# A gated convolution mixer on one core: the first filter half by column halves, one row block moved between filter loads

## The chip, the cores and the metric

The kernel runs on one core of a Trainium2 chip. The metric is device time in microseconds (us) of one launch. The engines are TensorE (PE, with its weight loads PEld), VectorE (DVE), ScalarE (ACT), GpSimd (POOL) and SyncE (SP); SP issues most of the DMAs, GpSimd the accumulating ones, ScalarE two small ones.

## What is computed

With S = 2048 rows and D = 640 columns, x = `A_q`:

```python
g = sigmoid((x * gate_w).sum(-1, keepdims=True))
# a: the gated long convolution
k_shift = sum_t k_pad[:, t:t+S] * shift_k[:, 3 - t]     # 4 taps
kv = k_shift * v
y  = irfft(rfft(kv_pad, 2S) * rfft(ssm_k_pad, 2S))[:S]  # per column
y  = y + kv * ssm_D
a  = x * y
# b: token-mixing MLP on the normalised rows
h = layernorm(x)
u = gelu(einsum("bsd,sf->bdf", h, w1) + b1)             # F = 1536
b = (einsum("bdf,fs->bds", u, w2) + b2).transpose
out = g * a + (1 - g) * b
```

All inputs and the output are bfloat16.

## The kernel before

**The convolution** is done with a short Fourier transform by matmuls. Rows are split by position into two halves (h = 0, 1) and four phases (p = 0 to 3). A transform of 1024 points becomes matmuls with cosine and sine tables `FTB[:, p, kt, c, k2, :]`, where c is the component (cosine or sine), k2 one of two blocks of frequencies and kt one of two blocks of 128 rows. The tables are made at the start: VectorE builds integer phases (`pint`, lines 801 to 808), ScalarE takes their sine (`sins`, line 810), one table of 1024 columns for each p, in the order 0, 2, 1, 3. Results lie in tiles `C[0..3]` and `SS` with four slots of `SL` = 2560 columns, a slot being (c, k2, 640 columns).

**The filter** `ssm_k` is stored by column of the model, so it is first transposed on TensorE: `transp(h, db)` (line 838) turns 128 of the 640 columns for one half, into one PSUM slot, and ScalarE evacuates the slot to `wT` (128x1024). Five of these (db = 0 to 4) make one half. Columns 0 to 319 of `wT` come from db = 0, 1 and 2. For h = 0, `fwd` (line 854) then makes, for every p, k2 and c, one group of four matmuls of 320 columns: two `kt`, each with the two column halves (`ci`) in the two halves of a PSUM slot. ScalarE evacuates each group (128x640) to `C[0]`. There are 16 such groups. Before each group of transposes of h = 0 TensorE does some matmuls on zeros (`spin`, `SPIN`), three more before the first group of `fwd`.

**The MLP** needs normalised rows. `X` holds `A_q` in four blocks of 640 KB (hk = 0 to 3), 16 tiles in all. VectorE takes statistics of each tile (`ln_tile`, line 913), GpSimd makes 1/sqrt of the variance for eight tiles at a time (`ln_scale`, line 926), VectorE applies it (`ln_apply`). The first MLP matmul (`m1`, line 1074; weights in `ring`) accumulates over hk, the second (`m2`, line 1112; weights in `W2`) fills the rest of the program. GpSimd also makes the tap matrices `KF` (line 971), four products that read `cw`, which ScalarE evacuates from a small transpose, and that are made to wait for the last integer phases of `pint` (`xr=[pv3]`).

**Later** the spectra of kv are multiplied by those of the filter (`product`, line 1138; `cross`, line 1178) on VectorE, with GpSimd's DMAs adding partial products in place, `invmix` mixes them for the inverse, and `inverse` (line 1209) multiplies by the inverse tables and by `A_q`. `q_hi` serves first as scratch for the products; afterwards the first 1024 rows of `A_q` are loaded into it anew (line 1262), as two DMAs of 640 KB. `q_lo` (line 1268) gets the other rows.

**What sets the order.** The program is written as a list of operations with read and write regions. A planner, `_Sched.run` (line 384), simulates the engines with durations given in the code (DMA: bytes by `rate`, 365 KB/us unless given, one transfer after another, plus 2 us) and picks on each free engine the ready operation with the lowest `prio` (its index in the program unless given). The order that comes out is emitted; each engine then runs its instructions strictly in that order, waiting on semaphores that `_Tracker` places from the regions touched. PSUM is four slots of two banks, `pp0` to `pp3`. A group takes a slot when its first matmul is planned (lines 450 to 453) and gives it back after its evacuation. The planner lets the convolution (`cv`) hold three at once and the MLP (`mlp`) two. Loads marked `chain=True` are issued by SP in program order (lines 765 to 817): the filter's h = 0 in three parts (256, 512 and 512 KB), X in four, small rows, the filter's h = 1, and then the ring and the key rows.

Of the kernel before, what the change touches and what calls it, by code (L numbers as in the profile page):

```python
# [18 lines left out]
class _Tracker:  # L19
# [230 lines left out]
        self.dma_sems[name] = sem  # L250
        self.dma_cnt[name] = 0

    def dma(self, stream, out_ap, in_ap, semname, transpose=False, noncontig=False, accum=False):
        reads = [in_ap] + ([out_ap] if accum else [])
        writes = [out_ap]
        acc = self.pre(stream, reads, writes)
        engobj = self.eng[stream]
        sem = self.dma_sems[semname]
        if transpose:
            ins = engobj.dma_start_transpose(out_ap, in_ap)  # L260
        elif accum:
            ins = engobj.dma_start(out_ap, in_ap, accum_op=ALU.add, max_dma_last_dim=2560)  # L262
        elif noncontig:
            with self.nc.allow_non_contiguous_dma(reason="tiny"):
                ins = engobj.dma_start(out_ap, in_ap)
        else:
            ins = engobj.dma_start(out_ap, in_ap)  # L267
        ins.then_inc(sem, 16)
        self.dma_cnt[semname] += 16
        v = self.dma_cnt[semname]  # L270
        self.dma_hist[(semname, v)] = dict(self.known[stream])
        src = ("dma", semname, v)
        for reg, mode in acc:
            self.add_record(reg, mode, src)
        return v
# [48 lines left out]
class _Sched:  # L324
# [59 lines left out]
    def run(self):  # L384
# [30 lines left out]
        while started < n:  # L415
            while frees and frees[0][0] <= t:
                _, sl, cls = heapq.heappop(frees)
                nfree.append(sl)
                held[cls] -= 1
            nxt = []  # L420
            progress = False
            for e in engs:
                while pend[e] and pend[e][0][0] <= t:
                    _, p, i = heapq.heappop(pend[e])
                    heapq.heappush(ready[e], (p, i))
                if free[e] > t:
                    nxt.append(free[e])
                    continue
                skipped = []
                pick = None  # L430
                while ready[e]:
                    p, i = heapq.heappop(ready[e])
                    op = ops[i]
                    if op.vt is not None and op.vt.slot is None:
                        c = op.vt.cls
                        if not nfree or held.get(c, 0) >= self.limit.get(c, 99):
                            skipped.append((p, i))
                            continue
                    pick = op
                    break  # L440
                for s in skipped:
                    heapq.heappush(ready[e], s)
                if pick is None:
                    if pend[e]:
                        nxt.append(pend[e][0][0])
                    continue
                op = pick
                progress = True
                started += 1
                if op.vt is not None and op.vt.slot is None:  # L450
                    nfree.sort()
                    op.vt.slot = nfree.pop(0)
                    held[op.vt.cls] = held.get(op.vt.cls, 0) + 1
                op.start = t
                if e in ("SP", "QA") or op.lat < 0:
                    issue = 1.2 if e == "POOL" else 0.1
                    s = max(t + issue, dma_free)
                    dma_free = s + op.dur
                    op.end = dma_free + 2.0 + (6.0 if e == "POOL" else 0.0)
                    free[e] = t + issue  # L460
                else:
                    op.end = t + op.dur
                    if op.lock:
                        op.end += max(port["POOL" if e == "DVE" else "DVE"] - t, 0.0)
                        port[e] = op.end
                    free[e] = op.end
                order.append(op)
                if op.vt is not None:
                    op.vt.left -= 1
                    if op.vt.left == 0:  # L470
                        heapq.heappush(frees, (op.end + 0.05, op.vt.slot, op.vt.cls))
                for s in op.asucc:
                    avail[s] = max(avail[s], op.start)
                    s.ndep -= 1
                    if s.ndep == 0:
                        heapq.heappush(pend[s.eng], (avail[s], s.prio, s.idx))
                for s in op.succ:
                    lat = 0.08 if s.eng == e else 0.15
                    if e == "PE" and s.eng == "PE":
                        lat = 0.0  # L480
                    avail[s] = max(avail[s], op.end + lat)
                    s.ndep -= 1
                    if s.ndep == 0:
                        heapq.heappush(pend[s.eng], (avail[s], s.prio, s.idx))
                nxt.append(free[e])
            if not progress:
                c = [x for x in nxt if x > t]
                if frees:
                    c.append(frees[0][0])
                assert c, "schedule stuck: " + str([(o.name, o.eng, o.ndep) for o in ops if not hasattr(o, "end")][:12])  # L490
                t = min(c)
# [19 lines left out]
def _build(nc, A_q, A_k, A_v, A_shift_k, A_ssm_k, A_ssm_D, B_x, B_w1, B_b1, B_w2, B_b2, gate_w, out):  # L511
# [6 lines left out]
    SL = 4 * D  # L518
# [3 lines left out]
    with ExitStack() as es:  # L522
# [179 lines left out]
        def dma(o, i, nbytes, stream="SP", prio=None, sem=None, rate=365.0, chain=False, **kw):  # L702
            if sem is None:
                sem = f"d{ndma[0]}"
                ndma[0] += 1
            if sem not in T.dma_sems:
                T.add_dma_sem(sem, es.enter_context(nc.semaphore(f"s_{sem}")))
            rd = [i] + ([o] if kw.get("accum") else [])
            o_ = SC.add(stream, nbytes / rate / 1000.0, lambda s: T.dma({"QA": "ACT"}.get(stream, stream), o, i, sem, **kw), rd, [o], prio=prio, lat=-1.0, name="dma")
            if chain:  # L710
                if last[0] is not None:
                    o_.after.add(last[0])
                last[0] = o_
            return o_

        def dr(t, off, ap):
            return bass.AP(tensor=t.tensor, offset=t.offset + off, ap=ap)
# [7 lines left out]
        def chk(ci):  # L725
            return lambda s: s[:, ci * 512:ci * 512 + 320]

        def ssm_load(h, a, b):
            dma(ssm[:, a:b, 1024 * h:1024 * h + 1024], dr(A_ssm_k, 128 * S * a + 1024 * h, [[S, 128], [128 * S, b - a], [1, 1024]]), 128 * (b - a) * 2048, chain=True)

        def row8(t, hk):
            return dr(t, (1024 * (hk // 2) + 4 * (hk % 2)) * D, [[8 * D, 128], [1, 4 * D]])
# [2 lines left out]
            return 16 + 128 * (1 - hk % 2)  # L735

        def x_load(hk):
            dma(X[:, hk, :, :], dr(A_q, 512 * hk * D, [[4 * D, 128], [1, 4 * D]]), 128 * 5120, chain=True)

        def w1_load(c, hk):  # L740
            dma(ring[c % 2][:, 4 * hk:4 * hk + 4, :], dr(B_w1, 512 * hk * F + 512 * c, [[4 * F, 128], [F, 4], [1, 512]]), 128 * 4096, chain=True)
# [24 lines left out]
        SSM1 = ((0, 2), (2, 5))  # L766
        small(Drow[:, :], dr(A_ssm_D, 0, [[0, 1], [1, D]]), 1280, "QA")
        small(rows[0:20, 0, 0:128], dr(A_shift_k, 0, [[128, 20], [1, 128]]), 5120, "QA")
        for a, b in SSM0:
            ssm_load(0, a, b)  # L770
        for hk in range(4):
            x_load(hk)
        small(rows[0:4, 1, :], dr(B_b2, 0, [[512, 4], [1, 512]]), 4096, "SP", chain=True)
        small(rows[0:12, 2, 0:128], dr(B_b1, 0, [[128, 12], [1, 128]]), 3072, "SP", chain=True)
# [4 lines left out]

        zz = alloc("zz", [128, 512], BF16, at=base_of(GTB))  # L780
        memset("DVE", zz[:, :], 0.0, prio=-1)
        SPIN = (6, 1, 1, 1, 1)

        def spin(k):
            return [((lambda s: s[:, 0:512]), zz[:, 0:128], zz[:, :], True, True)] * k
# [52 lines left out]
        def transp(h, db):  # L838
# [11 lines left out]
            o_ = act(V(wT, 2 * h * SL + 128 * db, [[SL, 2], [D, 4], [1, 128]]), (lambda s: s[:, :].rearrange("q (a b c) -> q a b c", a=2, b=4)), ACT.Copy, vt=vt, name="wT")  # L850
            if h == 0:
                o_.after.add(sins[0 if db == 0 else 2])

        def fwd(src, h, p, dst, slot, scale, name, neg=lambda c, k2: False):
            for k2 in range(2):
# [84 lines left out]
        lnlast = []  # L940
        kfirst = []
        KFP = (0, 5, 10, 15)
        srcW = lambda h: (lambda kt, p, ci: wT[:, 2 * h + kt, p, 320 * ci:320 * ci + 320])
        for h in range(2):
            for db in range(ND):
                transp(h, db)
            if h == 0:
                consts()
            if h in (1,):
                fwd_even(srcW(h), h, C[h], 1.0 / 1024.0, h == 1, "W")  # L950
            for p in (PORD if h not in (1,) else PORD[2:]):
                if h == 0 and p in (1, 3):
                    sins[p].prio = SC.ops[-1].idx - (16.5 if p == 1 else 8.5)
                fwd(srcW(h), h, p, C[h], p, 1.0 / 1024.0, "W", (lambda c, k2: False) if h == 0 else (lambda c, k2: c == 1))
            if h == 0:
                for t in range(8):
# [301 lines left out]
        lastp = []  # L1258
        chained(product, A1[1], A1[1], V0[1], tmp_of(q_hi, 0), V1[1])
        chained(product, A1[0], A1[0], V0[0], tmp_of(q_hi, 1), V1[0])  # L1260
        for kt in range(2):
            dma(q_hi[:, kt, :, :], dr(A_q, 512 * kt * D, [[4 * D, 128], [1, 4 * D]]), 128 * 5120)
        acc_dma(A1[1], V1[1])
        acc_dma(A1[0], V1[0])
        chained(product, A0[1], A0[1], V0[1], H(V0[1], 0))
        chained(product, A0[0], A0[0], V0[0])
        for kt in range(2):
            dma(q_lo[:, kt, :, :], dr(A_q, (1024 + 512 * kt) * D, [[4 * D, 128], [1, 4 * D]]), 128 * 5120).after.add(w2last)
# [41 lines left out]
```

## Time and profile before

| | |
|---|---|
| median of 4 runs | 185.02 us (184.11 to 186.54) |
| the profiled execution's own time | 184.11 us |
| its span in the trace | 182.2 us |
| TensorE, VectorE, ScalarE, GpSimd busy | 172.9, 171.6, 117.4, 39.1 us |
| DMA | 43.49 MB, mean 239 GB/s |
| chain that ended last | PE 84%, ACT 10%, DMA 3% |

The span runs from the first to the last event of the trace; the 1.9 us beside it are before and behind. Busy shares are means over stages with different limits, so they only say which engines to look at. The order of time and the table of stretches say which of them a stage waits for. In the trace's rows, `L293` is the helper line for every matmul, `L669` for every ScalarE operation, `L625` for every two-input VectorE or GpSimd operation, so the tiles (out<-in) tell what an operation is. A row's bracket is the engine's idle time ahead of it and what ended it.

### The profile page before, as it was taken

Reading aid. Unit: us, or ns where it says so; the run is one execution under the profiler, and the core shown is the slowest. Engines: PE = TensorE matmul, PEld = TensorE weight load, DVE = VectorE, ACT = ScalarE, POOL = GpSimd, SP = SyncE. Lnnn points to the kernel's source line nnn. Section 1 sums busy time; section 2 is a strip of 40 time slices with the busy share of each in tenths; the row PEclk is TensorE's granted clock in tenths of the full one; section 3 lists DMA queues with packets and bytes.
Section 4 is the critical chain, followed back from the end, with each engine's and each line's share of the span. In section 5 each row is a group of like instructions: output and inputs, shape, how many; then the busy total and the mean of one; then the engine's idle time right before and its main releaser. Section 6 shows DMA issues by size and latency. Waiting matters only on the chain.

```text
span 182.2 us, 3317 instructions
## 1 busy us (share of the span) xinstructions
PE 172.9 (95%) x1373; PEld 126.7 (70%) x1374; DVE 171.6 (94%) x203; ACT 117.4 (64%) x176; POOL 39.1 (21%) x42
## 2 busy tenths in 40 slices
PE   7978998979999999999999999999999999999991
PEld 2644584576778777776777778888888887678670
DVE  7799895999999999999998999999999999999875
ACT  5799988799989988149999941231322313761660
POOL 4059704000000055000510110402535000054000
PEclk9999999999999999999999999999999999999999
DMA  5999999999999989997499969699999998279484
GB/s 157 391 414 371 389 250 226 305 415 263 160 249 290 163 214 229 240 230 170 117 237 251 275 151 342 149 222 335 226 192 253 245 207 241 117 113 237 82 288 144
DMA packets 38541, 43.49 MB, mean 239 GB/s; under 512 B 15867, under 2 KB 31360, under 8 KB 38528
## 3 DMA queue, kind: packets, MB, share of 16 engines
q1 hardware_dynamic: 33296, 32.16, 59.6%
q0 software_dynamic: 5200, 11.14, 34.6%
q8 instruction: 10, 0.16, 0.3%
q10 hardware_dynamic: 32, 0.01, 0.0%
q14 instruction: 3, 0.02, 0.0%
HBM read 25.87 MB, written 2.62 MB: 156 GB/s over the span
## 4 chain that ended last, share of the span: by engine, by line
PE 84%; ACT 10%; DMA 3%; DVE 1%; issue 0%; DVEq 0%; SPq 0%
PE pp L293 84%; ACT C L669 4%; DMA ssm<-in_A_ssm_k_dram 3%; ACT wT L669 2%; ACT FTB L669 1%; ACT L669 1%; ACT ksh L669 1%; DVE cgb L625 0%; ACT cgb L669 0%; ACT GT L669 0%; DVE O L681 0%; DVE O L625 0%; DVEq L504 0%; SPq L267 0%; DVE cgb L639 0%
## 5 line engine op out<-in xcount | busy, mean ns | idle before, releaser
L625 DVE TENSOR_TENSOR C<-C 128x2560 bf16<-128x2560 bf16 (+2 forms) x37 | 54.6, 1521 | 0.8 <-DMA C<-SS 0.4
L293 PE MATMUL pp<-X,ring 128*128 128x320 bf16 x384 | 55.3, 299 | 0.0
L293 PE MATMUL pp<-GT,W 128*128 128x320 bf16 x384 | 52.8, 299 | 0.0
L293 PEld LDWEIGHTS pp<-GT,W 128*128 128x128 bf16 x384 | 43.4, 113 | 8.8 <-ACT cgb L669 0.2
L293 PEld LDWEIGHTS pp<-X,ring 128*128 128x128 bf16 x384 | 37.0, 98 | 15.1 <-DVE X L640 0.7
L669 ACT ACTIVATE C<-pp 128x640 bf16<-128x640 f32 x64 | 40.1, 725 | 5.4 <-PE pp L293 5.4
L669 ACT ACTIVATE O<-pp,c,omg 128x640 bf16<-128x640 f32 x15 | 13.3, 886 | 33.8 <-PE pp L293 33.8
L262 POOL DMA_DIRECT2D C<-C x8 | 10.9, 1611 | 46.5 <-DVE C L625 46.0
L293 PE MATMUL pp<-wT,FTB 128*128 128x320 bf16 x112 | 17.8, 300 | 1.6 <-ACT C L669 1.6
L669 ACT ACTIVATE cgb<-pp,gg 128x640 bf16<-128x640 f32 x16 | 12.7, 794 | 8.3 <-PE pp L293 8.3
L293 PEld LDWEIGHTS pp<-wT,FTB 128*128 128x128 bf16 x112 | 9.5, 98 | 8.8 <-ACT C L669 5.2
L919 DVE BATCH_NORM_STATS2 stats<-X 128x6 f32<-128x320 bf16 x32 | 13.7, 463 | 1.4 <-DMA X<-in_A_q_dram 1.4
L669 ACT ACTIVATE GT<-pp,cc 128x640 bf16<-128x640 f32 x12 | 9.4, 784 | 8.3 <-PE pp L293 8.2
L625 DVE TENSOR_TENSOR tm<-C,C 128x2560 bf16<-128x2560 bf16 (+1 forms) x7 | 14.3, 2057 | 0.0
L293 PE MATMUL pp<-C,FTB 128*128 128x320 bf16 x96 | 13.6, 299 | 0.0
L262 POOL DMA_DIRECT2D C<-q_hi x6 | 5.9, 977 | 31.2 <-DVE C L625 16.2
L293 PEld LDWEIGHTS pp<-C,FTB 128*128 128x128 bf16 x96 | 9.0, 98 | 4.1 <-ACT O L669 0.2
L669 ACT ACTIVATE gq<-gq 128x640 bf16<-128x640 bf16 x16 | 11.6, 729 | 0.3 <-DVE gq L625 0.3
L625 DVE TENSOR_TENSOR SS<-C 128x2560 bf16<-128x2560 bf16 x8 | 11.7, 1486 | 0.1
L625 DVE TENSOR_TENSOR C<-tm 128x2560 bf16<-128x2560 bf16 (+1 forms) x9 | 10.7, 1193 | 0.1
L669 ACT ACTIVATE wT<-pp 128x1024 bf16<-128x1024 f32 x10 | 9.5, 1034 | 1.2 <-PE pp L293 1.2
L293 PE MATMUL pp<-KF,KT 128*128 128x128 bf16 (+1 forms) x160 | 9.0, 213 | 1.2 <-ACT GT L669 1.1
(73 smaller groups left out, 186.8 us busy)
## 6 DMA issues: line engine op xcount, KB each, us to landing
ring<-in_B_w_dram SPq DMA_DIRECT2D x12, 512.0 KB, 10.2
W<-in_B_w_dram SPq DMA_DIRECT2D x12, 512.0 KB, 7.2
C<-C POOLq DMA_DIRECT2D x8, 640.0 KB, 11.5
X<-in_A_q_dram SPq DMA_DIRECT2D x4, 640.0 KB, 8.6
kn<-in_A_k_dram SPq DMA_DIRECT2D x4, 640.0 KB, 9.4
out_dram<-O SPq DMA_DIRECT2D x7, 320.0 KB, 2.8
C<-SS POOLq DMA_DIRECT2D x3, 640.0 KB, 11.7
ssm<-in_A_ssm_k_dram SPq DMA_DIRECT2D x3, 512.0 KB, 5.9
```

Of the source, the lines that this page charges most:

```text
L262: ins = engobj.dma_start(out_ap, in_ap, accum_op=ALU.add, max_dma_last_dim=2560)
L293: ins = self.nc.tensor.matmul(ps_ap, lhsT=lhsT, rhs=rhs, start=start, stop=stop, skip_group_check=True)
L625: o_ = SC.add(eng, d, lambda s: T.op(eng, lambda e: e.tensor_tensor(o, a, b, op), rd, [o]), rd, [o], prio=prio, name="tt")
L669: return T.op("ACT", lambda e: e.activation(o, src, func, **kw), rr + [src], ww)
L919: ops.append(SC.add("DVE", 0.38, (lambda o, i: lambda s: T.op("DVE", lambda e: e.bn_stats(o, i), [i], [o]))(o, i), [i], [o]))
```

## The change

1. The planner takes free PSUM slots in the order in which they came free; the list is no longer sorted.
2. In the chain of loads, block 0 of X is moved ahead of the last part of the filter's h = 0. The planner's rates for these loads are given anew (262 and 195 KB/us for the parts of h = 0, 385 for h = 1, 410 for X).
3. The filter's h = 0 goes through a new function, `fwd_c`: for each column half `ci`, each p and each k2, a group of four matmuls puts the two components c into the two halves of a PSUM slot, and one evacuation writes both. The loop over `ci` is outermost. `fwd` still serves h = 1.
4. Transposes db = 3 and 4 of h = 0, with their evacuations, and the sines of p = 1 and 3 get priority 0.
5. `SPIN` goes from (6, 1, 1, 1, 1) to (7, 3, 3, 2, 2).
6. The reload of `q_hi` is placed behind the product of `A0[1]` and waits for what is written to that tile's second component.

```diff
-    def dma(self, stream, out_ap, in_ap, semname, transpose=False, noncontig=False, accum=False):
-        reads = [in_ap] + ([out_ap] if accum else [])
+    def dma(self, stream, out_ap, in_ap, semname, transpose=False, noncontig=False, accum=False, wait=()):
+        reads = [in_ap] + ([out_ap] if accum else []) + list(wait)
...
                 if op.vt is not None and op.vt.slot is None:
-                    nfree.sort()
                     op.vt.slot = nfree.pop(0)
...
         def ssm_load(h, a, b):
-            dma(ssm[:, a:b, 1024 * h:1024 * h + 1024], dr(A_ssm_k, 128 * S * a + 1024 * h, [[S, 128], [128 * S, b - a], [1, 1024]]), 128 * (b - a) * 2048, chain=True)
+            dma(ssm[:, a:b, 1024 * h:1024 * h + 1024], dr(A_ssm_k, 128 * S * a + 1024 * h, [[S, 128], [128 * S, b - a], [1, 1024]]), 128 * (b - a) * 2048, chain=True, rate=(262.0 if a == 0 else 195.0) if h == 0 else 385.0)
...
         def x_load(hk):
-            dma(X[:, hk, :, :], dr(A_q, 512 * hk * D, [[4 * D, 128], [1, 4 * D]]), 128 * 5120, chain=True)
+            dma(X[:, hk, :, :], dr(A_q, 512 * hk * D, [[4 * D, 128], [1, 4 * D]]), 128 * 5120, chain=True, rate=410.0)
...
-        for a, b in SSM0:
+        for a, b in SSM0[:2]:
             ssm_load(0, a, b)
-        for hk in range(4):
+        x_load(0)
+        ssm_load(0, *SSM0[2])
+        for hk in range(1, 4):
             x_load(hk)
...
-        SPIN = (6, 1, 1, 1, 1)
+        SPIN = (7, 3, 3, 2, 2)
...
+        def fwd_c(p, ci, dst, scale):
+            for k2 in range(2):
+                vt = _VT("cv")
+                items = []
+                for kt in range(2):
+                    for c in range(2):
+                        items.append((chk(c), FTB[:, p, kt, c, k2, :], srcW(0)(kt, p, ci), kt == 0, kt == 1))
+                m_ = mms(vt, (spin(3) if (p, ci, k2) == (1 if EVH else 0, 0, 0) else []) + items, name="W")
+                m_.dur = 0.54
+                act(V(dst, p * SL + k2 * D + 320 * ci, [[2 * D, 2], [1, 320]]), two, ACT.Copy, vt=vt, name="We", scale=scale)
+
+        EVH = False
...
+        DB3 = 0
+        SINP = {1: 0, 3: 0}
...
                 transp(h, db)
+                if h == 0 and db > 2:
+                    for o_ in SC.ops[-2:]:
+                        o_.prio = DB3
...
-            for p in (PORD if h not in (1,) else PORD[2:]):
-                if h == 0 and p in (1, 3):
-                    sins[p].prio = SC.ops[-1].idx - (16.5 if p == 1 else 8.5)
+            if h == 0:
+                for ci in range(2):
+                    for p in PORD:
+                        fwd_c(p, ci, C[0], 1.0 / 1024.0)
+                for p in (1, 3):
+                    sins[p].prio = SINP[p]
+            for p in (() if h == 0 else PORD[2:]):
                 fwd(srcW(h), h, p, C[h], p, 1.0 / 1024.0, "W", (lambda c, k2: False) if h == 0 else (lambda c, k2: c == 1))
...
-        for kt in range(2):
-            dma(q_hi[:, kt, :, :], dr(A_q, 512 * kt * D, [[4 * D, 128], [1, 4 * D]]), 128 * 5120)
         acc_dma(A1[1], V1[1])
         acc_dma(A1[0], V1[0])
         chained(product, A0[1], A0[1], V0[1], H(V0[1], 0))
+        for kt in range(2):
+            dma(q_hi[:, kt, :, :], dr(A_q, 512 * kt * D, [[4 * D, 128], [1, 4 * D]]), 128 * 5120, wait=[H(A0[1], 1)])
         chained(product, A0[0], A0[0], V0[0])
```

More of the change, by code (lines that the diff above doesn't have):

```diff
@@ L707, in dma @@
                 T.add_dma_sem(sem, es.enter_context(nc.semaphore(f"s_{sem}")))
-            rd = [i] + ([o] if kw.get("accum") else [])
+            rd = [i] + ([o] if kw.get("accum") else []) + list(kw.get("wait", ()))
             o_ = SC.add(stream, nbytes / rate / 1000.0, lambda s: T.dma({"QA": "ACT"}.get(stream, stream), o, i, sem, **kw), rd, [o], prio=prio, lat=-1.0, name="dma")
```

## The prediction, before the changed kernel was run

> **What bounds the kernel now.** I read the page from the top, then the chain of waits, then a table of stretches cut where the matmul stream changes its nature, then VectorE, ScalarE and GpSimd in order of time over the first 40 us. First the page, busy shares:
>
> ```profile
> PE 172.9 (95%) x1373; PEld 126.7 (70%) x1374; DVE 171.6 (94%) x203; ACT 117.4 (64%) x176; POOL 39.1 (21%) x42
> ```
>
> TensorE and VectorE are both nearly full, so the few microseconds in which they stand still are what can be won. The chain of waits says where:
>
> ```profile
> 5.82 1.99 PE pp L293 x25
> 8.12 3.66 ACT wT L669 x4
> 11.79 1.03 ACT FTB L669
> 12.82 2.97 ACT C L669 x5
> 16.47 1.03 ACT FTB L669
> 18.15 11.44 PE pp L293 x102
> 38.81 137.71 PE pp L293 x1084
> ```
>
> From 38.81 us to 176.52 us it is one unbroken run of matmuls. Everything before it is a mixed start-up in which ScalarE (evacuations wT and C, sines FTB) sets the pace. The table of stretches (columns: stretch, length, then busy time and count of PE, PEld, DVE, ACT, POOL, granted clock, DMA share, GB/s):
>
> ```profile
> 5.80:11.40 5.60, 4.45 (x47) 3.26 (x49) 4.17 (x10) 5.01 (x7) 0.17 (x1) 1.00 1.00 410
> 11.40:22.10 10.70, 9.99 (x70) 5.47 (x69) 10.11 (x37) 10.70 (x19) 10.07 (x7) 1.00 1.05 386
> 22.10:29.10 7.00, 7.00 (x75) 5.80 (x73) 7.00 (x20) 6.04 (x8) 0.00 (x0) 1.00 1.12 259
> 29.10:38.80 9.70, 7.56 (x74) 4.50 (x72) 7.56 (x15) 8.12 (x12) 2.39 (x4) 1.00 1.03 303
> 38.80:176.50 137.70, 137.69 (x1086) 104.74 (x1087) 134.84 (x109) 83.65 (x131) 24.33 (x21) 1.00 0.95 219
> ```
>
> In 11.4 to 22.1 ScalarE is busy for all of it: the filter's first half is evacuation-bound. In 29.1 to 38.8 TensorE loses 9.70 - 7.56 = 2.14 us. After that it loses nothing, so a gain must be made before 38.8, by moving matmul work forward into the start, and it must not be lost again at the end. VectorE in order of time shows what holds the start:
>
> ```profile
> 9.26 0.49 DVE L919 BATCH_NORM_STATS2 stats<-X 128x6 f32<-128x320 bf16 x1 [1.36 <-DMA X<-in_A_q_dram]
> 10.40 0.68 DVE L639 TENSOR_SCALAR pint<-pint 128x1024 int32<-128x1024 int32 x1
> 21.38 2.23 DVE L640 TENSOR_SCALAR X<-X,mv,rstd 128x640 bf16<-128x640 bf16 x6 [0.56 <-POOL rstd L625]
> 31.52 2.94 DVE L640 TENSOR_SCALAR X<-X,mv,rstd 128x640 bf16<-128x640 bf16 x8 [2.11 <-POOL rstd L625]
> ```
>
> and GpSimd in order of time:
>
> ```profile
> 11.23 8.12 POOL L625 TENSOR_TENSOR KF<-cw,m 128x1120 bf16<-128x1120 bf16 x4 [8.44 <-DVE pint L639]
> 19.34 0.25 POOL L639 TENSOR_SCALAR sd<-mv 128x8 f32<-128x8 f32 x1
> ```
>
> The reader is to see a relay. VectorE waits 1.36 us for the first row block, with the last two integer operations of the phase table (pint) queued behind that wait. GpSimd's four tap products start only when the second of those is done (11.08), run 8.12 us, and the row statistics' root queues behind them (19.34 to 21.34), so VectorE waits another 0.56 us. The MLP matmuls can begin only at 22.27, and the second batch of rows is normalised only from 31.52.
>
> **The change part by part.**
>
> *Row block before the last filter load.* Before, X block 0 landed at 9.26 with 256 + 512 + 512 + 640 KB sent; the 768 KB ahead had landed at 5.77. That is 1152 KB in 3.49 us, 330 KB/us (estimate from these two landings). Block 0 moved ahead of the last 512 KB lands at about 5.77 + 640/330 = 7.7 us, and the third filter load at about 9.3. VectorE ends its previous operation at 7.89, so the 1.36 us go. The bytes ahead of every later load are the same, and SP issues the same number of descriptors, so blocks 1 to 3 and all weights land as before. Next in line: pint's end moves from 11.08 to about 9.3, the tap products to 9.4 to 17.5, the root to 17.5 to 19.4. Statistics for eight tiles (0.86 us each) are then ready at 17.65 - 1.36 = 16.3, and all twelve at about 19.4, so the 0.56 us go as well. First rows normalised at 19.5 rather than 21.38, second batch at 29.6 rather than 31.52. **VectorE is 1.9 us earlier.** The 2.11 us behind the second root stay: nothing else is ready there.
>
> *Column halves, both components per evacuation.* Counted: 16 groups of four 320-column matmuls and 16 evacuations of 128x640 as before; every matmul already has its own weight load (112 and 112). An evacuation stays at about 0.61 us (6.07 us for 10), a group of matmuls at 0.54. So zero of itself. What it does: the first half needs only the transposed columns 0 to 319, that is three of five transposes, so ScalarE has C work while the late third load arrives. Without this the block swap would cost: wT 3 and 4 can't be evacuated before 9.3 + 0.7. ScalarE's work from 5.18 to 23.45 is 18.27 us with one hole of 0.59 us (waiting for the tap transposes); it is conserved. The sines for the odd tables (1.15 us each) move to the front and can fill that hole: -0.6 to 0; I take -0.2.
>
> *Spins.* 17 in place of 10. The first extra one is cold: six took 2.74 us, so +0.43 us before the first transposes if the first filter rows are already there (their load is shown to land 2.7 us after issue, about 3.5); 0 to +0.4 on ScalarE's start. The others (0.22 us warm) sit where TensorE waits for data or slots (0.49 and 0.65 us at 9.4 and 10.9). I take +0.3 for all.
>
> *Slots in turn.* Before, the lowest free slot is taken, so three of four serve the filter. In turn, TensorE may run one evacuation further ahead: it can leave the evacuation-bound stage up to 0.6 us earlier, and a wait such as 1.07 us for the first gelu's slot (at 37.3) may fall on an older slot. Bounds: +0.5 (an in-order engine meets a slot freed later) to -1.6; by the nearer row, the group, I take -0.3.
> Here a rule speaks against the change. TensorE's row: 4.29 us for 28 matmuls from 18.15, with 0.21 us stops at each slot, at granted clock 1.00, 153 ns each. The Trainium skill, "TensorE: Matmul & The Clock Gate", section "A second HAM failure mode: psum-queue depth-cycling", says that cycling through PSUM banks each iteration makes the array stop briefly often enough that its clock swings between half and full. If it did, a group would take 1.08 us in place of 0.54, above the 0.61 of the evacuation: +0.47 x 16 = 7.5 us. By the trace, which already cycles three slots at full clock, 0. I take 0.
>
> *q_hi reloads later.* The two 640 KB loads were issued at 122.4 and 133.0; now both wait for the accumulate that C[1]'s second component gets. That was issued at 135.26 and takes 11.7 us (page, C<-SS), so they are issued at about 147. Queued behind them on SP is only q_lo (was 149.97, used at 170.9); the last W2 load (132.42) is ahead. Earlier loads took 3.6 to 10.7 us, giving 150.6 to 157.7 against first use at 158.04: hidden, with 0.3 to 7 us to spare. On the other side 1.28 MB leaves the window of the accumulates; the wait that it could shorten is 0.41 us on VectorE at 146.8, off TensorE's chain. I take 0; bounds -0.4 to +1.
>
> **Sum.** -1.9 (VectorE) -0.2 (sines) +0.3 (spins) -0.3 (slots) = -2.1 us. Does TensorE get all of it? The MLP matmuls of the first batch (34 until 29.1) start up to 1.9 us earlier but the array is full in 22.1 to 29.1. What pays is the second batch, ready at 29.6 instead of 31.5, just as TensorE begins to idle: of the 2.14 us lost there most are fillable. VectorE is moved as much, so the end, where the inverse follows VectorE by 0.9 us (first group 167.61, its input written by about 166.7), keeps its distance. Profiled execution 184.11 (span 182.2 plus 1.9) becomes 182.0; the median of the runs is 0.9 above it, so **182.9 us**.
>
> **Rivals.**
> - *Forecast, 0.50*: 182.9, own range 181.9 to 183.9 (half of the 2.1 us unfilled, or the gelu wait gone too).
> - *Absorbed, 0.24*: VectorE is early, but TensorE between 29 and 39 is paced by ScalarE (8.12 of 9.70 busy; two-matmul groups at 0.62 us each; a 1.28 us table load at 35.16), and only 0.3 to 0.8 us come through: 184.5. For it: four of the waits there are for C and for GT. Against: the array had no MLP work left just then.
> - *More, 0.05*: both the hole and the gelu wait close: 180.5.
> - *A wait in TensorE's fixed order, slower, 0.21*: the planner now believes 410 KB/us for row blocks, and places MLP groups from about 19.5 us between the filter's groups. If the tap products start as late as before (their taps' evacuation cw queued behind a sine, or behind the longer spins), rows are ready at 21.4 still. TensorE then stands 1.9 us with filter groups behind it, ScalarE starves once its stock of three groups (1.8 us) is used, and the second half's transposes and the second batch move too: +2 to +4 us, 187 to 189. It decides if the first normalised row comes over 0.6 us (a group) after its place in the order. The statement for it: 8.12 us of GpSimd work leave no slack before 19.34. A landing of q_hi past 160 would end alike and is counted here.
> - *That it doesn't do what it says*: the loads are chained in program order, so the swap is certain; I see none.
>
> **How the numbers follow.** What a measurement of this kernel can tell from no change is about 1%, 1.85 us; faster means below 183.17. Of the forecast's 0.50 about 0.41 lies below that and 0.09 above; with "more" 0.46 faster. Same: 0.09 + 0.24 = 0.33. Slower: 0.21. The range leaves out about a tenth at each end: 181.2 (past the forecast's own low end) to 187.2 (into the slow case).
>
> **What would show it.** Right: VectorE's first statistics before 8 us with no wait for X; tap products from about 9.4; first normalising near 19.5 and second near 29.6; unbroken matmuls from about 37 rather than 38.8. Wrong: ScalarE idle before 12 us (column halves don't cover the late load), TensorE waiting for X or the ring near 20 us, a wait for q_hi's load near 156 us, or the unbroken run starting at 38.8 again.

## The result, and the profile after

The changed kernel takes 184.34 us (median of 43 runs, 183.70 to 185.15), the kernel before 185.02 (64 runs beside them, 183.61 to 187.12). The ratio is 0.9962 [0.9949, 0.9976]: faster by 0.4%, clear of zero, and well short of the 1.1% that were forecast. The profiled executions are nearer still: 183.99 us after, 184.11 before, both with a span of 182.2.

Busy time of the engines, from the page of the kernel after:

```profile
PE 173.4 (95%) x1380; PEld 129.0 (71%) x1381; DVE 171.1 (94%) x203; ACT 117.1 (64%) x176; POOL 41.3 (23%) x42
```

TensorE is busy 0.5 us more, with seven matmuls more (the spins); GpSimd 2.2 us more, VectorE 0.5 and ScalarE 0.3 us less. The table of stretches, with the cuts of before:

```profile
5.80:11.40 5.60, 4.09 (x37) 2.46 (x37) 5.54 (x15) 5.60 (x8) 1.62 (x1) 1.00 1.02 413
11.40:22.10 10.70, 10.70 (x87) 7.23 (x85) 10.11 (x36) 10.07 (x18) 8.62 (x7) 1.00 1.05 384
29.10:38.80 9.70, 8.67 (x92) 6.07 (x91) 7.92 (x13) 8.63 (x12) 3.69 (x3) 1.00 1.01 263
38.80:176.50 137.70, 136.79 (x1073) 104.53 (x1070) 133.96 (x109) 82.84 (x132) 24.29 (x21) 1.00 0.93 220
```

From 29.1 to 38.8 TensorE is busy 1.11 us longer than before (8.67 against 7.56). In the last stretch, which lost nothing before, it now loses 0.91 us. VectorE in order of time:

```profile
19.94 2.94 DVE L639 TENSOR_SCALAR X<-X,mv,rstd 128x640 bf16<-128x640 bf16 x8 [0.56 <-POOL rstd L624]
30.07 2.94 DVE L639 TENSOR_SCALAR X<-X,mv,rstd 128x640 bf16<-128x640 bf16 x8 [2.11 <-POOL rstd L624]
...
143.74 4.30 DVE L624 TENSOR_TENSOR C<-C 128x2560 bf16<-128x2560 bf16 x3
147.95 1.49 DVE L624 TENSOR_TENSOR SS<-C 128x2560 bf16<-128x2560 bf16 x1
...
152.44 1.49 DVE L624 TENSOR_TENSOR SS<-C 128x2560 bf16<-128x2560 bf16 x1 [1.61 <-DMA C<-C]
153.85 4.29 DVE L624 TENSOR_TENSOR C<-C 128x2560 bf16<-128x2560 bf16 x3
```

and GpSimd:

```profile
9.78 8.13 POOL L624 TENSOR_TENSOR KF<-cw,m 128x1120 bf16<-128x1120 bf16 x4 [7.00 <-DVE pint L638]
17.89 0.25 POOL L638 TENSOR_SCALAR sd<-mv 128x8 f32<-128x8 f32 x1
```

The relay moved as foreseen: tap products 1.45 us earlier (9.78 for 11.23), normalising 1.44 us earlier (19.94 for 21.38; 30.07 for 31.52). The wait of 0.56 us for the root stayed. At the other end a wait of 1.61 us for an accumulating DMA is new; the one of before was 0.41 us, at another step:

```profile
144.91 1.49 DVE L625 TENSOR_TENSOR C<-C 128x2560 bf16<-128x2560 bf16 x1
146.82 7.10 DVE L625 TENSOR_TENSOR C<-C 128x2560 bf16<-128x2560 bf16 x5 [0.41 <-DMA C<-SS]
153.84 1.49 DVE L625 TENSOR_TENSOR SS<-C 128x2560 bf16<-128x2560 bf16 x1
```

VectorE reaches this place 1.17 us earlier (143.74 for 144.91), but its order has changed. `invmix` of the second half writes to `SS`. Two such steps (147.95 and 152.44) now stand among those of the first half, and the second of them needs the last accumulate. Before, the first step into `SS` stood behind all five into `C`. ScalarE over the first 24 us:

```profile
5.34 1.02 ACT L668 ACTIVATE wT<-pp 128x1024 bf16<-128x1024 f32 x1 [0.76 <-PE pp L293]
...
12.48 1.02 ACT L668 ACTIVATE wT<-pp 128x1024 bf16<-128x1024 f32 x1 [0.41 <-PE pp L293]
13.73 1.02 ACT L668 ACTIVATE wT<-pp 128x1024 bf16<-128x1024 f32 x1 [0.22 <-PE pp L293]
...
17.06 6.73 ACT L668 ACTIVATE C<-pp 128x640 bf16<-128x640 f32 x11
```

It begins 0.16 us later than before (5.18), stands still for 0.41 and 0.22 us until the last two groups of transposes are done (those of the third load), and ends the filter's first half at 23.79 (before: 23.45). TensorE:

```profile
10.50 0.72 PE L293 MATMUL pp<-wT,FTB 128*128 128x320 bf16 x4 [1.51 <-ACT wT L668]
...
16.59 5.66 PE L293 MATMUL pp<-wT,FTB 128*128 128x320 bf16 x40
22.14 1.25 PE L293 MATMUL pp<-X,ring 128*128 128x320 bf16 x8
...
107.50 43.63 PE L293 MATMUL pp<-GT,W 128*128 128x320 bf16 x320
158.29 2.33 PE L293 MATMUL pp<-C,FTB 128*128 128x320 bf16 x16 [0.62 <-DVE C L624]
...
176.22 1.79 PE L293 MATMUL pp<-GT,W 128*128 128x320 bf16 x12
```

and in the kernel before:

```profile
22.27 1.25 PE L293 MATMUL pp<-X,ring 128*128 128x320 bf16 x8
...
108.28 44.72 PE L293 MATMUL pp<-GT,W 128*128 128x320 bf16 x328
...
158.26 4.58 PE L293 MATMUL pp<-C,FTB 128*128 128x320 bf16 x32
...
176.34 1.79 PE L293 MATMUL pp<-GT,W 128*128 128x320 bf16 x12
```

Three times of TensorE tell the story. I call the first **T0**, the end of the filter's first half on TensorE: 22.14 us, 22.27 before. The second is the first m2 matmul: 107.50, 108.28 before. The third is the last m2 group: 176.22, 176.34 before. So the start is where it was, 0.65 us are won between T0 and m2, and 0.62 of the 0.78 in hand are lost at 158.29, where TensorE waits for VectorE. The chain of waits shows behind what:

```profile
135.54 16.44 DMA C<-C
...
152.44 0.98 DVE SS L624
...
153.85 4.30 DVE C L624 x3
...
158.29 18.10 PE pp L293 x132
```

One accumulate of 640 KB takes 16.44 us to land. That is not new: of the three accumulates issued in this window the slowest takes 16.4 us in the kernel before too, and the quickest 9.7 us where it took 11.5. What is new is that a step which needs the slowest stands ahead of those that TensorE waits for.

The profiles explain 0.12 us of the 0.68 between the medians. Much of the rest is in the spread: 28 of the 64 runs of before are above 185.15 us, none of the 43 after. The other 36 of before have a median of 184.59, only 0.25 above the median after (a cut at the highest run of after can only narrow the difference).

### The profile page after: what moved, and what is told of

Its sections match the earlier page's. It is cut to its first block, busy times and chain, and to the rows that moved or that the text cites. A ratio compares the mean times of both kernels' runs of the same rounds, so it can differ in the third digit from the quotient of the medians.

```text
span 182.2 us, 3334 instructions
## 1 busy us (share of the span) xinstructions
PE 173.4 (95%) x1380; PEld 129.0 (71%) x1381; DVE 171.1 (94%) x203; ACT 117.1 (64%) x176; POOL 41.3 (23%) x42
## 4 chain that ended last, share of the span: by engine, by line
DVE 47%; PE 24%; ACT 13%; DMA 9%; issue 5%; POOL 1%; DVEq 0%
DVE C L624 31%; PE pp L293 24%; DMA C<-C 9%; ACT gq L668 4%; DVE tm L624 4%; ACT FTB L668 2%; DVE q_hi L624 2%; DVE SS L624 2%; ACT C L668 2%; DVE gq L624 2%; DVE vkv L624 2%; DVE kv L624 2%; ACT wT L668 2%; ACT GT L668 1%; DVE kp L749 1%
## 5 line engine op out<-in xcount | busy, mean ns | idle before, releaser
L293 PE MATMUL pp<-wT,FTB 128*128 128x320 bf16 x112 | 17.3, 300 | 2.4 <-ACT wT L668 1.5
L293 PEld LDWEIGHTS pp<-wT,FTB 128*128 128x128 bf16 x112 | 10.3, 98 | 7.7 <-ACT C L668 2.1
L668 ACT ACTIVATE gq<-gq 128x640 bf16<-128x640 bf16 x16 | 11.7, 732 | 0.6 <-DVE gq L624 0.6
L262 POOL DMA_DIRECT2D O<-q_hi x4 | 4.8, 1200 | 28.4 <-DVE q_hi L624 28.4
```

The lines of the kernel that those rows point to most:

```text
L293: ins = self.nc.tensor.matmul(ps_ap, lhsT=lhsT, rhs=rhs, start=start, stop=stop, skip_group_check=True)
L668: return T.op("ACT", lambda e: e.activation(o, src, func, **kw), rr + [src], ww)
```

## The experiments

Ratios are to the kernel before, with 95% intervals. Most edits are to the kernel after. Three readings in competition: G, that the later reload of `q_hi` gives time back at the end; that the gain was never made, since the start is paced by ScalarE and its order; and W, that the moment at which the array reaches full speed decides.

**The end.** e1 puts the reload back:

```diff
+        for kt in range(2):
+            dma(q_hi[:, kt, :, :], ...)
         acc_dma(A1[1], V1[1])
...
-        for kt in range(2):
-            dma(q_hi[:, kt, :, :], ..., wait=[H(A0[1], 1)])
```

> The changed kernel with the q_hi reload back at its old place. Theory G (given back late): the reload, now issued at 143.9 us into the same window as the accumulates, makes the accumulate C<-C land late (152.0) and costs TensorE 0.62 us at 158.3; with the reload earlier that wait goes and the time is 183.6 to 183.9. Theory S (spread): the old reload, issued into the accumulates between 122 and 133 us, is what puts a share of the runs of before above 185.2; then this kernel has that upper group again and its median is 184.8 to 185.3. Theory N: the reload does nothing and the time stays at 184.2 to 184.5.

0.9992 [0.9959, 1.0025], 184.87 us (184.37 to 188.24). With the old place TensorE still waits 1.04 us for VectorE's C (at 152.41) and VectorE 1.08 us for an accumulate. G falls as the account of a loss: the later reload costs nothing and may be worth 0.3% (the intervals overlap). Four of the 14 runs are at 187.2 to 188.2, and their cause was not traced; without them the median is 184.65. The edit changes more than the load: VectorE's order at the end is that of before again, as in every profile with the old place (before, e1, e4, e8, e16). The changed order comes with the later place (e2, e3 and e6 have it too). Each order has its wait for an accumulate.

e5 keeps `q_lo` out of the window of the accumulates:

```diff
-            dma(q_lo[...], ...).after.add(w2last)
...
         Z1 = invmix(A1[0], A1[1], (SS, 0), None, None)
+            dma(q_lo[...], ..., wait=[V(C[3], 0, [[1, SL]])]).after.add(w2last)
```

> The changed kernel, the same order of instructions, but the two q_lo loads (1.28 MB, issued at 147.05 us) wait for VectorE's fourth inverse-mixing step on the second half. Theory: they share the DMA engines with the last accumulates, which land at 152.0 and hold VectorE 1.6 us and TensorE 0.62 us. Then both waits shrink and the ratio to the kernel before is 0.991 to 0.994. Rival: the accumulates are slow of themselves (their own queue), then the wait stays and the ratio is that of the changed kernel, 0.995 to 0.998, or worse if q_lo comes too late for its use at 170.8.

0.9968 [0.9946, 0.9990]. VectorE's wait for the accumulate is 1.55 us and TensorE's 0.57, and the slowest accumulate takes 16.4 us again: it is not slow because of this load.

e14 leaves out the last two accumulates (the sum of `V1[0]` into `A1[0]` is missing from the output):

```diff
-        acc_dma(A1[0], V1[0])
```

> The changed kernel without the last two accumulating DMAs of 640 KB (C<-C into A1[0]); the output leaves their sum out. If VectorE's wait for their landing (1.6 us at 150.8) is what makes TensorE stand 0.62 us at 158.3, both waits go and the time falls by 0.5 to 0.8 us against the changed kernel: ratio 0.991 to 0.994. If TensorE's wait there has another cause, it stays: 0.996.

1.0108 [1.0067, 1.0150]. The planner changed the order of VectorE's steps and issued the two loads of `q_lo` at 132.44 us, just ahead of the accumulate that is left there. This one then takes 13.4 us (9.7 in the changed kernel), VectorE waits 2.31 us for it and TensorE 2.27. So e14 does not isolate what it was made for. e11 tells the planner that accumulates take longer (in the kernel of e9, below):

```diff
-                    op.end = dma_free + 2.0 + (6.0 if e == "POOL" else 0.0)
+                    op.end = dma_free + 2.0 + (8.0 if e == "POOL" else 0.0)
```

> As e9, with the planner's latency of an accumulating DMA at 8 us in place of 6 (they take 10 to 16). The start keeps its order; TensorE gets 16 more second-MLP matmuls ahead of the first inverse, so it should no longer wait for VectorE near 157 us (0.6 to 1.1 us in the others). If that wait was what gave part of the lead back, the ratio is 0.003 to 0.006 below e9's; if the end is VectorE's chain (rival), it is the same as e9's or above.

1.0066 [1.0037, 1.0094]. The wait near 157 us is gone, but now all of m2 is done before the last inverse and nothing fills the gaps of the tail, and VectorE waits 1.57 us for `q_hi`. A gain of a microsecond ahead of 150 us is thus not simply passed on to the end. That VectorE's order and its accumulates set the time there is read from the traces; no run changes them alone.

**Slots in turn.** e2 sorts the free list again:

```diff
+                    nfree.sort()
                     op.vt.slot = nfree.pop(0)
```

> The changed kernel with the free slots sorted again. If the turn of slots gave TensorE its missing wait for the first gelu (1.07 us at 37.3 before, none after), it comes back and the time is 184.9 to 185.4. If it was the earlier rows that closed it (rival), 184.2 to 184.6.

1.0096 [1.0065, 1.0126], 187.38 us. TensorE in order of time in e2:

```profile
6.27 0.82 PE L293 MATMUL pp<-zz 128*128 128x512 bf16 x3 [1.11 <-ACT wT L669]
...
23.22 1.25 PE L293 MATMUL pp<-X,ring 128*128 128x320 bf16 x8
```

The second transposes get the slot of the first, so TensorE stands 1.11 us until ScalarE has emptied it; T0 is 1.08 us later than after. With this start, slots in turn are worth 1.3% (1.0096 against 0.9962). The profile is of e2's lower group of runs (8 at 185.3 to 186.2); the 14 above 187.2 have no profile, so the wait of 1.11 us explains only part of the 1.3%. e4 is e2 with the reload of e1, which leaves the start of the change alone:

> The kernel before with the start alone (load order, column halves, spins, priorities, rates). VectorE should be 1.4 us early at its second normalising (about 30.1 us). If the start carries the gain: 184.1 to 184.5, if it is the slots and the reload: 184.8 to 185.3.

1.0129 [1.0067, 1.0191], 187.84 us (6 runs). T0 is 25.05: the same wait of 1.11 us, and in its profile the array went on at half speed for some 3 us behind it (eight transposes took 1.07 us at 8.30 and 0.71 at 10.45). VectorE has no lead here: the tap products start only at 11.83, behind the late evacuation of `cw`, and the second batch is normalised at 32.12, not at the expected 30.1.

e3 is the kernel before with the two other parts, slots in turn and the later reload:

> The kernel before with the slots in turn and the later reload, without anything of the start (load order, column halves, spins, priorities). If the start carries the gain: 184.8 to 185.3. If the gain is the slots and the reload, as theory S has it: 184.1 to 184.5.

0.9995 [0.9970, 1.0019]: nothing. So the slots and the reload together are worth nothing to the old start (that neither does anything alone is not shown), and the new start needs the slots.

**The start, part by part.** e6 takes the row block back behind the filter loads:

```diff
-        for a, b in SSM0[:2]:
+        for a, b in SSM0:
             ssm_load(0, a, b)
-        x_load(0)
-        ssm_load(0, *SSM0[2])
-        for hk in range(1, 4):
+        for hk in range(4):
             x_load(hk)
```

> The changed kernel with the row blocks behind all three filter loads again, all else kept. VectorE should wait for X again (about 1.4 us) and normalise the second batch at about 31.5. If VectorE's lead is what TensorE gained from (the prediction's step), the unbroken run of matmuls starts 1.5 to 2 us later and the ratio is 1.003 to 1.008. If ScalarE paces TensorE there (rival), 0.995 to 0.999.

0.9922 [0.9899, 0.9946], 183.58 us: faster than the whole change. ScalarE in e6, then TensorE:

```profile
11.28 1.95 ACT L668 ACTIVATE wT<-pp 128x1024 bf16<-128x1024 f32 x2
...
16.08 6.74 ACT L668 ACTIVATE C<-pp 128x640 bf16<-128x640 f32 x11
```

```profile
21.17 1.22 PE L293 MATMUL pp<-ident,ssm 128*128 128x128 bf16 x16
...
157.52 2.33 PE L293 MATMUL pp<-C,FTB 128*128 128x320 bf16 x16 [1.08 <-DVE C L624]
```

The two holes in front of the last transposes are gone, the last C evacuations start 0.98 us sooner, T0 is 21.17, m2 begins at 106.30. The expected loss on VectorE did not come: it normalises at 19.70 and 30.49. The planner, which now takes the block to be later, put the last `pint` ahead of the statistics. The relay was freed by VectorE's order; the swap of the loads was not needed for it, and held up the transposes. The rates given anew are kept in e6, and by them the planner expects the block later than by the old ones; no run leaves them out, so their share in VectorE's order is not shown. Of the 1.20 us in hand at m2 against the whole change, 0.46 go into a longer wait for VectorE (1.08 for 0.62), and 0.70 come through (183.29 against 183.99 in the profiled executions).

e7 puts back 10 spins for 17:

```diff
-        SPIN = (7, 3, 3, 2, 2)
+        SPIN = (6, 1, 1, 1, 1)
```

> The changed kernel with the ten spins of before. If the spins only cost time, as the prediction has it, 0.3 us less: ratio 0.993 to 0.996. If they keep the array's clock from coming up late (theory W: where TensorE stood still at 5 to 7 us, in the sorted kernels, matmuls stayed at half speed until 9 us), some runs are 1 to 2 us longer, the spread grows past 2 us, and the median is 185 or more.

0.9915 [0.9889, 0.9942], 183.48 us. T0 is 21.49: the seven spins cost 0.65 us there. The lead is still 0.65 at m2 (106.85) and 0.35 at the last m2 group (175.87), since TensorE's wait for VectorE's C grows from 0.62 to 0.92 us. e8 adds them to the kernel before:

> The kernel before with the seventeen spins alone. By the cost alone 0.3 us more: ratio 1.001 to 1.003. By theory W the group of longer runs of before (above 185.2) goes and the ratio is 0.994 to 0.998. If with sorted slots the spins wait for the evacuation of the first transposes (1.1 us, as in the sorted kernels), 1.004 to 1.012.

1.0005 [0.9977, 1.0033]. T0 is 23.30 in its profile, 1.03 us later than before. Its 14 runs lie between 184.53 and 186.01, the 54 of the kernel before beside them between 183.91 and 187.09. That would fit spins that are dearer at best and cheaper at worst, but the extremes of so few runs don't show it.

e9 is e6 and e7 together:

> The changed kernel with both the row blocks behind the filter loads and the ten spins, so with slots in turn, sines and transposes early, column halves and the later reload. Theory T: the end of the filter's first half on TensorE (T0: 22.14 us in the changed kernel, 21.17 with the old load order, 21.49 with the old spins), paced by ScalarE, carries over to the end, and VectorE's lead doesn't. Then T0 is 20.5 to 20.9 and the ratio 0.985 to 0.990, less what VectorE's wait for the accumulates near 157 us takes (it grew to 1.08 us as TensorE got earlier), so 0.988 to 0.992. Rival, the prediction's step: the load order is what gives the gain, then 0.996 or more.

0.9953 [0.9921, 0.9984]: the gains do not add. Its runs fall into two groups, 9 at 182.99 to 183.44 and 11 at 184.18 to 185.67. Its profile is of the lower group, and even there the array is late:

```profile
6.35 1.07 PE L293 MATMUL pp<-ident,ssm 128*128 128x128 bf16 x8 [0.57 <-DMA ssm<-in_A_ssm_k_dram]
```

Eight transposes take 1.07 us here and at 8.00, and 0.72 at 9.99; in e6 and e7 they take about 0.7 from 6.0 on. T0 is 21.43, no earlier than in e6: what the fewer spins save is lost again at half speed.

e10 is e9, e12 the kernel after, without column halves:

```diff
-                for ci in range(2):
-                    for p in PORD:
-                        fwd_c(p, ci, C[0], 1.0 / 1024.0)
+                for p in PORD:
+                    fwd(srcW(h), h, p, C[h], p, 1.0 / 1024.0, "W")
```

> As e9, with the filter's first half by components again (no column halves). In e9 no evacuation of C stands before the last of wT, so the column halves should give nothing there: T0 within 0.3 us of e9's and a ratio within 0.003 of it. Rival: they are worth something of their own (1 us).

> The changed kernel by components (no column halves), all else kept, the row block still ahead of the third filter load. The prediction says that the swap would cost without the halves, since ScalarE has no C work until the late load is transposed: T0 0.6 to 1 us later than 22.14, ratio 1.000 to 1.005. If the halves do nothing here either: 0.995 to 0.998.

e10 is 0.9989 [0.9958, 1.0021], e12 0.9913 [0.9877, 0.9949] (183.87 us, 9 runs). So column halves seem to gain 0.4% with the block behind the filter (e9 against e10; the intervals overlap), and cost 0.5% with the block ahead of it (after against e12; the intervals just touch, and by the medians it is 0.25%), the very case in which I had called them needed. In e12 TensorE does wait 1.02 us for the third load, but its last two groups of transposes start at 9.97 and 11.20, and T0 is 21.37. In the kernel after a W group (four filter matmuls) with a wait of its own of 1.51 us (at 10.50) stands in front of the last two, and they start at 11.74 and 12.97. Behind T0 the profile of e12 doesn't show the gain: it is the slowest of its nine runs (184.42), with m2 at 108.04 and a wait of 1.83 us for VectorE's C.

**VectorE's lead by itself.** e13 is the kernel after with one statistics instruction done six times, which makes VectorE 2.1 us late and leaves all orders as they are:

```diff
+                nx = 6 if (t, ci) == (1, 1) else 1
-                ops.append(... T.op("DVE", lambda e: e.bn_stats(o, i), [i], [o]) ...)
+                ops.append(... [T.op("DVE", lambda e: e.bn_stats(o, i), [i], [o]) for _ in range(nx)] ...)
```

> The changed kernel with one row statistic (0.43 us) done six times in place of once, early on VectorE, every engine's order unchanged. VectorE then normalises at about 21.4 and 31.6 us, as before the change, while the end of the filter's first half on TensorE (T0, 22.14) can't move. If VectorE's lead was on the path, as the prediction has it, its 1.5 us come back as 1.3 to 1.5 us: ratio 1.003 to 1.005 to before. If T0 alone counts, 0 to 0.3 us: 0.996 to 0.998. Between: the part that came through.

> The changed kernel once more, beside e13, e14 and the kernel before on the same chip: 0.995 to 0.998, all runs within about 1.5 us of each other.

e13 is 1.0010 [0.9987, 1.0033], 184.90 us; e15, the kernel after beside it, 0.9965 [0.9938, 0.9993], 184.33 us. VectorE in e13, then TensorE:

```profile
22.08 2.89 DVE L639 TENSOR_SCALAR X<-X,mv,rstd 128x640 bf16<-128x640 bf16 x8
...
32.15 2.94 DVE L639 TENSOR_SCALAR X<-X,mv,rstd 128x640 bf16<-128x640 bf16 x8 [2.11 <-POOL rstd L624]
```

```profile
108.65 43.63 PE L293 MATMUL pp<-GT,W 128*128 128x320 bf16 x320
```

With VectorE 2.1 us later TensorE is 1.23 us later at m2 (107.42 in e15); 0.34 of that are not VectorE's, since the array reached full speed later in this profile (the last 40 filter matmuls start at 16.86, 16.52 in e15). That leaves 0.89. The run is 0.57 us longer by the medians and 0.83 by the ratios (0.0045 x 185). So a microsecond of VectorE's lead is worth about 0.3 to 0.4 of one at the end, less if the late full speed is in the other runs of e13 too. The two kernels don't overlap: the lowest run of e13 is at 184.76, the highest of e15 at 184.42.

**The same kernel, profiled again.** e16 is the kernel before, unchanged, one execution:

> A second look at the kernel before. Theory W: its runs spread over 3 us because the array comes to full speed at a moment that varies (the first matmuls on zeros take 0.43 us each, later ones 0.21); in this look the change falls at another time than 5.5 us, and T0 and the span move with it. If T0 is the same (22.3) and the span differs, the spread comes from elsewhere.

185.97 us, from the upper group. TensorE in order of time in e16:

```profile
11.30 1.07 PE L293 MATMUL pp<-ident,ssm 128*128 128x128 bf16 x8
12.17 1.48 PE L293 MATMUL pp<-zz 128*128 128x512 bf16 x3
...
23.93 1.25 PE L293 MATMUL pp<-X,ring 128*128 128x320 bf16 x8
```

and, from the first profile of the same kernel:

```profile
5.82 0.71 PE L293 MATMUL pp<-ident,ssm 128*128 128x128 bf16 x8
```

Eight transposes take 1.07 us at half speed and 0.71 at full. The first profile is at full speed by 5.82 us, e16 only from about 13.4, behind the row at 12.17. From the second group on the transposes come later (the last start at 11.30 for 9.57), T0 by 1.66 us (23.93 for 22.27), the time by 1.86 (185.97 for 184.11). For this execution W is shown. That the upper group of before as a whole is of this kind is inferred from it alone.

## Why the prediction was wrong

It forecast 182.9 us, a gain of 2.1; the median gain is 0.68, and 0.12 in the profiles. The time lies in the stated range, which is 6 us wide, and beside the rival called "absorbed" (184.5), whose mechanism was half of it: W groups do wait for ScalarE between 29 and 32 us, but most of what came through was lost at the end.

- **The step that failed is the first term of the sum**, "VectorE is 1.9 us earlier", counted in full as TensorE's. It was too large by a slip: the wait that goes is 1.36 us, but the end of pint was moved by 1.8 (11.08 to 9.3). In the rows of before pint ends 1.82 us behind the first statistic (9.26 to 11.08); from 7.89 that gives 9.7, and 9.62 was measured. So the tap products end where the root starts (17.89), not at 17.5, the wait of 0.56 us for the root stayed, and VectorE came 1.44 us earlier. And the lead pays 0.3 to 0.4 of itself at the end (e13 against e15). In the trace: after T0 the first m1 groups stand where they stood (22.14), and the second batch is met only behind three W groups paced by ScalarE, at 31.77 rather than 32.11. Of the 2.14 us that TensorE lost from 29.1 to 38.8, 1.11 were filled. The wait of 1.07 us for the first gelu's slot is gone, but not by the lead: in e13, with VectorE 2.1 us later, it doesn't come back, only 0.16 us for X do (at 32.75). e3, with the slots in turn but the old start, keeps it, so it went with the order of the new start. "The unbroken run starts at about 37" held (from 35.84 there are only stops of 0.15 and 0.16 us until 158.29).
- "The end keeps its distance" failed. The distance was read at the inverse group of 167.61; TensorE lost 0.62 of its 0.78 us at the earlier one of 158.29. VectorE's lead of 1.17 us there was used up: it waited 1.61 us for an accumulate in place of 0.41. The accumulate is issued earlier with VectorE and takes as long as before (16.4 us); what had not been foreseen is that VectorE's order would change so that it is needed earlier. This is read from the traces. No run isolates it, so how much of the lead another order of the end would pass on stays open.
- **Of the load swap I costed only the gain**, and took its cost to be covered. With the third load later the planner put a waiting group ahead of the last transposes, and ScalarE got two holes of 0.63 us together. Undoing it gains 0.4% (0.9922 against 0.9962). The sign to look for was in the text ("ScalarE idle before 12 us"); the cover that I had named, column halves, is what e12 seems to do better without.
- **Spins**: +0.3 taken, +0.65 at T0 measured (e7). I had put all but the first into TensorE's waits; the waits in front of the transposes had been closed by the slots.
- **Slots in turn**: -0.3 taken. With the old start, and the reload beside them, nothing (e3), with this one 1.3%, 2.5 us (e2 against after), beyond my bound of -1.6: what I had weighed was an older slot in the evacuation-bound stage, and what it does is to spare the second transposes a wait of 1.11 us at the very start. In e2's profile that is 1.54 us at the last m2 group (177.76); the rest lies in its upper group, which has no profile.
- **Column halves**: 0 taken; plus 0.5% or minus 0.4% by the order of loads (e12; e9 against e10), both at the edge of what the runs can tell.
- **Reload of q_hi**: 0 taken, some -0.3% measured (e1), with the order of the end that comes with it. It lands in time. It was issued at 143.88, not 147, since the accumulate that it waits for took 9.7 us, not 11.7.
- **The clock**: that cycling the slots would not slow the array was right (40 matmuls in 5.66 us, 142 ns each). What I left out is when it becomes fast at all: I read one profile of before, at full speed by 5.8 us, as its usual start, while 28 of 64 runs lie above all runs after.
- The sines' -0.2 was to come from a hole of 0.59 us that is gone, with two others in its place; it was not measured alone.
- A small misreading: the MLP matmuls until 29.1 are 32 in the trace, not 34. Nothing rests on it.

The sum by terms, at T0: spins +0.65 and load swap +0.97, each from its undoing (they don't add in e9), against what slots, order and halves brought, gave 22.14 for 22.27. Behind T0 0.65 us were won by the lead and the order; the end took back 0.62.

Three versions are faster than both kernels, each the change with one part undone: by component (0.9913, its interval just touching that of the change), 10 spins (0.9915), block behind the filter (0.9922). Their intervals overlap. Two undone together are 0.9953. In e9's profile, of its lower group, they don't because the array is late; for its upper group, which has no profile, this is open.

## What to carry to other kernels

A wait removed from an engine that runs beside the bounding one is worth what the bounding engine can use of it: delay that engine alone by as much and see what the end does, before counting the lead in full. When a load is moved ahead, cost the one that it displaces, and ask whether another order on the engine would have freed the same relay. When an engine comes early to the end, check which step it will then wait at: a planner may have put another one first. And look at a kernel's runs as a distribution: here more of the difference lies in one kernel's upper group than in the two profiles.

## What the hardware showed that was not expected

- The same kernel reached full speed of the array by 5.8 us in one execution and at about 13.4 in another, 4.6 and 12.2 us after its first matmul at 1.18. The Trainium skill, "TensorE: Matmul & The Clock Gate", Part 1, gives about 4 us of sustained activity, give or take 0.5; the first agrees (4.6 is the latest that it can be), e16 does not, and here the measurement decides. e4 and e9 lie between, at full speed by 10.3 and 9.8 us.
- Why e16 was late isn't told by its stops. Before full speed it has stops of 0.19 us (at 5.97) and 0.36 us (at 11.09). e10 stops for 0.66 us at the same place as the first of these, and is at full speed at 6.44 (eight transposes in 0.71 us). The stops of 0.49 and 0.65 us in the first profile come after full speed and don't end it.
- The row of granted clock reads 1.00 in both, so it doesn't show the half speed; the duration of matmuls of one shape does.
- An accumulating DMA of 640 KB within SBUF took up to 16.4 us in both kernels, and taking `q_lo`'s load out of its way did not shorten it (e5). The first of the three at the end took 9.7 us with no row load issued beside it, 11.5 and 12.2 with one of 640 KB issued at 133.0 and 132.35 (before, e1), and 13.4 with two issued at 132.44 (e14).
